# Three small edits around the second batch of a fused attention and gated-unit kernel: GpSimd makes the low part of Q, a product starts on three pairs of heads, a score buffer ends earlier

## The chip, the cores and the metric

One core of a Trainium2 chip. The time is device microseconds of one execution. The kernel before was run three times: 1341.32, 1342.89 and 1348.61 us, median 1342.89.

## The reference

Attention over 8 batches, 8 heads, 576 tokens, 64 features a head, in which only scores within `tau` of the row's maximum count; its output, 4608 tokens of 512 features, goes into a gated unit with 1536 inner features.

```
scores = q @ k.T / sqrt(64)
scores = where(scores >= max(scores) - tau, scores, -1e9)
x      = softmax(scores) @ v            # per batch and head, then heads side by side
gate   = sigmoid(x @ w_gate)
out    = (gate * (x @ w_val)) @ w_out
```

## The kernel before, in words

**Planner.** The kernel is a list of operations (`op`), each with an engine, an assumed cost, a key and the buffers it reads and writes. `Plan.run` (a list scheduler, executed while the program is built) lets every engine take the ready operation with the lowest key for which `room` finds free buffers; the instructions are then emitted in that order, so each engine's queue is fixed before the chip runs. `SLOTS` says how many buffers a tag has. An operation may also be tied `behind` another (it may be placed only once that one has been placed).

**Attention.** A visit is one pair of heads of one batch (8 batches of 4 pairs, 32 visits; counted from 0: pair 4 is the first pair of the second batch). A visit has nine score tiles: scores on PE (L653 or L661), maximum on DVE (L668), threshold on GpSimd or DVE (L677), exponential on ACT (L682), masking with the sum on DVE (L685), transposes on PE (L767) copied out of PSUM by ACT (L718), then the output product (L803). The first four pairs (`plain_scores`) use plain fp32. From pair 4 on (`split_scores`) K and Q are split in a rounded high part and the rest: ACT rounds K (L576) and scales and rounds Q (L578), GpSimd subtracts for K (L580), DVE for Q in one pass that scales and subtracts (L583). The parts are sent by SP into per-head tiles (`kd`, `qd`).

**Gated unit.** The output of a visit is split again (`split_x`, ACT L813 and GpSimd L815). When the four pairs of a batch are there, `in_units` computes 24 sums (12 blocks of gate and of value) of twelve matmuls each (four pairs of heads, three products each: L863), and `out_units` computes the second product (L906) with streamed weights (L841). A sum is issued in six chunks of two matmuls. Their keys start at 1e6, behind all attention. `FIRST_PAIRS` is the number of pairs that a chunk waits for at least: at 4 every chunk waits for all. The first three batches go through these two; the other five and a block of all leftover tokens are taken two at a time after attention (L1105, L1170), in a form with seven instead of eight products.

**Weights.** `convert` loads a piece of weights (SP, L473, L475), rebuilds its bits on GpSimd, ACT and DVE (L483, L487, L490, L496), and splits it (ACT L508, GpSimd L514). It shares the engines with attention until about 220 us.

**PSUM.** Eight banks: three double ones for scores (banks 0-1, 2-3, 4-5), two single ones (6, 7) for transposes, leftover keys, outputs and conversions. With the flag `active["moe"]` the third score buffer is given up and banks 4 and 5 become single banks; `started` sets it when the first product of the gated unit (key 1e6) is placed. While attention is active, the unit's sums may hold two single banks, attention two, conversions one.

Of the kernel before, what the change touches and what calls it, by code (L numbers as in the profile page):

```python
# [13 lines left out]
AF = mybir.ActivationFunctionType  # L14
ALU = mybir.AluOpType
# [5 lines left out]
def f32(ap):  # L21
    return ap.bitcast(F32)
# [21 lines left out]
class Plan:  # L44
# [51 lines left out]
        return o  # L96

    def room(self, o):
        need = {}
        for b in o.bufs + o.also:  # L100
            if b.tag in self.slots and not b.held:
                need.setdefault((b.tag, b.cls), set()).add(b)
        for (tag, cls), s in need.items():
            if len(s) + sum(len(x) for (t, c), x in need.items() if t == tag and c != cls) + self.held.get(
                tag, 0
            ) > self.slots[tag] - o.leave:
                return False
            cap = self.cap(tag, cls)
            if cap is not None and self.held.get((tag, cls), 0) + len(s) > cap:
                return False  # L110
            if tag in self.IN_TURN and any(b.turn != self.given.get(tag, 0) + 1 for b in s):
                return False
        if not self.settle([b for s in need.values() for b in s]):
            return False
        for s in need.values():
            for b in s:
                b.held = True
                self.given[b.tag] = b.turn
                self.held[b.tag] = self.held.get(b.tag, 0) + 1
                self.held[b.tag, b.cls] = self.held.get((b.tag, b.cls), 0) + 1  # L120
        return True

    def cap(self, tag, cls):
        return None

    def settle(self, bufs):

# [100 lines left out]
    "w": 9, "t2": 6,  # L228
}
LEAD = 8  # L230
CONV_IN, CONV_OUT = (24, 3), (56, 3)


# [48 lines left out]
def LATE(b, hp):  # L282
    return hp != 3

FIRST_PAIRS = 4
KD_COST = 1.2

TWOS = ((3, 4), (5, 6), (7, 8))
# [1 line left out]
SUMS_IN, SUMS_OUT, SUM_KEY = {1: (0,), 2: (1,)}, {0: (0,), 1: (1,)}, 300  # L290
# [8 lines left out]
def act(n):  # L299
    return 0.19 + 0.0008 * n  # L300
# [6 lines left out]
def pool(n):  # L307
    return 0.2 + 0.0022 * n


def mm(n):
    return 0.014 + 0.000418 * n
# [3 lines left out]
def kernel(  # L316
# [25 lines left out]
    nc = tc.nc  # L342
# [10 lines left out]
    SM = NJ * P  # L353
    SL = S - SM
    HALF = S // 2
    NF = DFF // P
    ND = DM // P
    NFG = NF // ND
# [24 lines left out]
    scale_t = cp.tile([P, 1], F32, tag="scale", name="scale_t")  # L383
# [16 lines left out]
    class Both(Plan):  # L400
# [23 lines left out]
                return more[0]  # L424
            return ps

        def started(self, o):
            if o.key == 1e6:
                active["moe"] = 1
            if o is last_att[0]:  # L430
                active["att"] = 0

# [2 lines left out]
    op, buf = plan.op, plan.buf  # L435
# [21 lines left out]
    def convert(i, f, key):  # L457
# [7 lines left out]
        raw = buf("w", [P, DM, 2], I32, f"wr{name}")  # L465
# [5 lines left out]
        def load():  # L471
# [4 lines left out]
                    out=raw.ap.rearrange("p f t -> p (f t)"), in_=w_out[f * P : (f + 1) * P, :]  # L476
                )

        op("SP", 1.6, key - 6, load, writes=[raw], leave=3)
        lo, hi = (lambda: raw.ap[:, :, 0]), (lambda: raw.ap[:, :, 1])  # L480

        bt = buf("b", [P, DM], F32, f"wb{name}", "conv")
# [1 line left out]
            out=at.ap.bitcast(F32), in0=hi().bitcast(F32), scalar1=zero_t[:, 0:1], scalar2=zero_t[:, 0:1],  # L484
# [44 lines left out]
    class Visit:  # L529
# [32 lines left out]
        def split_scores(self, key, n):  # L562
            b, hp = self.b, self.hp

            kn = buf("kn", [P, SK], F32, f"kn{n}")
            op("SP", 1.2, key - 6, lambda: nc.sync.dma_start(out=kn.ap, in_=k[b, hp]), writes=[kn])


            c0, c1 = self.c0, self.c1 + (2 * SL if self.with_left else 0)
            W, WM = c1 - c0, self.c1 - self.c0  # L570
            qn = buf("qn", [P, W], F32, f"qn{n}")
            op("SP", 1.2, key - 6, lambda: nc.sync.dma_start(out=qn.ap, in_=q[b, hp, :, c0:c1]), writes=[qn])


            k2 = self.k2 = buf("k2", [P, 2, SK + P], F32R, f"k2{n}")
            op("ACT", 0.73, key, lambda: nc.scalar.copy(k2.ap[:, 0, :SK], kn.ap), reads=[kn], writes=[(k2, 0)])  # L576
            q2 = self.q2 = buf("q2", [P, 2, W], F32R, f"q2{n}")
            op("ACT", act(W), key, lambda: nc.scalar.activation(q2.ap[:, 0], qn.ap, AF.Copy, scale=scale_t[:, 0:1]),  # L578
               reads=[qn], writes=[(q2, 0)])
            op("POOL", pool(SK), key, lambda: nc.gpsimd.tensor_tensor(  # L580
                out=k2.ap[:, 1, :SK], in0=kn.ap, in1=f32(k2.ap[:, 0, :SK]), op=ALU.subtract
            ), reads=[kn, (k2, 0)], writes=[(k2, 1)])
            op("DVE", 1.4 * W / 640, key, lambda: nc.vector.scalar_tensor_tensor(  # L583
                out=q2.ap[:, 1], in0=qn.ap, scalar=scale_t[:, 0:1], in1=f32(q2.ap[:, 0]), op0=ALU.mult, op1=ALU.subtract
            ), reads=[qn, (q2, 0)], writes=[(q2, 1)])
            self.WM = WM
            self.kd, self.qd = {}, {}
            for h in range(2):
                kd = self.kd[h] = buf("kd", [P, 2, SK], F32R, f"kd{n}_{h}")
                qd = self.qd[h] = buf("qd", [P, WM], F32R, f"qd{n}_{h}")  # L590
                own, other = slice(h * D, (h + 1) * D), slice((1 - h) * D, (2 - h) * D)
                for z, rows in enumerate((own, other)):
                    op("SP", 0.5, key + h, lambda qd=qd, rows=rows, own=own, z=z: nc.sync.dma_start(
                        out=f32(qd.ap[rows]), in_=f32(q2.ap[own, z, :WM])
                    ), reads=[(q2, z)], writes=[(qd, z)])
                for rows in (own, other):
                    op("SP", KD_COST, key + h, lambda kd=kd, rows=rows, own=own: nc.sync.dma_start(
                        out=f32(kd.ap[rows]), in_=f32(k2.ap[own, :, :SK])
                    ), reads=[k2], writes=[(kd, rows.start)])
# [228 lines left out]

    seq = [0]

    def moe_pe(cost, emit, reads, writes, also=()):
        seq[0] += 1
        return op("PE", cost, 1e6 + seq[0] - 1, emit, reads=reads, writes=writes, also=also)

    unit_ends = []

# [53 lines left out]

    def out_units(blk, g):

        two = blk in SUMS_OUT
        for es in ((0, 2), (1, 3)) if two else ((0,), (1,), (2,), (3,)):
            accs = {e: buf("b", [P, SM], F32, f"o{blk}_{e}", "moe") for e in es}
            outs = {e: buf("t2", [P, SM], F32, f"ot{blk}_{e}") for e in es}
            for fg, e in itertools.product(range(NFG), es):
# [4 lines left out]
                for j in range(0, 12, 2):  # L902
                    def go(j=j, w=w, fg=fg, acc=acc):
                        wv = w.ap.rearrange("p (f z c) -> p f z c", f=ND, z=2)
                        for f, a, z in ms[j : j + 2]:
                            nc.tensor.matmul(  # L906
                                acc.ap, wv[:, f, a], g[fg * ND + f].ap[:, z],
                                start=(fg, f, a, z) == (0, 0, 0, 0),
                                stop=(fg, f, a, z) == (NFG - 1, ND - 1, 1, 0),
                            )  # L910

                    fs = sorted({fg * ND + f for f, _, _ in ms[j : j + 2]})
                    end = moe_pe(2 * mm(SM), go, [g[f] for f in fs] + [w], [acc], also=[o] if fg == NFG - 1 else [])
                unit_ends.append(end)
                if e in SUMS_OUT.get(blk, ()):
                    first = w
# [470 lines left out]
```

## Time and profile before

| | |
|---|---|
| median of three runs | 1342.89 us (1341.32 to 1348.61) |
| profiled execution: span, first to last instruction | 1340.2 us (its device time is not given) |
| PE busy | 1314.8 us, 98% |
| DVE busy | 944.4 us, 70% |
| ACT busy | 727.8 us, 54% |
| GpSimd (POOL) busy | 492.7 us, 37% |
| DMA | 318.72 MB, mean 238 GB/s |

How to read it: PE is TensorE, PEld its weight loads, SPq the issuing of transfers. A row of a timeline is start (us), duration (us), engine, line, operation, output <- inputs, shapes, count merged in the row, and in brackets how long the engine was idle before it and what ended that. A row of the stage view is the stretch, its length, then for each engine busy us and number of instructions, and at its end the granted clock of TensorE as a share, the DMA share and GB/s. Matmuls are pipelined, so that neighbouring rows of PE overlap by some tenths.

### The profile page before, as it was taken

How to read it: one execution, taken by the hardware profiler on the slowest of the kernel's cores; microseconds unless marked ns; L12 is line 12 of the kernel's file. 1: busy time of each engine (PE TensorE's matmuls, PEld its weight loads, DVE VectorE, ACT ScalarE, POOL GpSimd, SP SyncE). 2: the span in 40 equal slices, each digit the busy share in tenths (PEclk: the TensorE clock that was granted, in tenths of full speed). 3: DMA queues.
4: the chain of work that ended last, by engine and by line, in shares of the span. 5: the costliest groups of instructions: out<-in, count | busy, mean ns of one | idle time of the engine just before them, and what ended most of it. 6: DMA issues, size and time to landing. Idle time of an engine off the chain costs nothing.

```text
span 1340.2 us, 23378 instructions
## 1 busy us (share of the span) xinstructions
PE 1314.8 (98%) x8292; PEld 1077.3 (80%) x8292; DVE 944.4 (70%) x1868; ACT 727.8 (54%) x1339; POOL 492.7 (37%) x474
## 2 busy tenths in 40 slices
PE   8889999999999999999999999999999999999998
PEld 5558887888888888888888888888888888888887
DVE  7888888777787776776777763556955569554594
ACT  8887777667767766666666652223522235322242
POOL 3576867724455363456464441110001010001100
PEclk9999999999999999999999999999999999999999
DMA  8889998999798888998988957656686566756563
GB/s 298 240 260 311 321 259 263 269 260 288 198 254 259 239 241 244 260 293 230 264 246 259 236 190 267 221 191 207 211 286 196 189 204 206 247 178 204 190 217 117
DMA packets 148115, 318.72 MB, mean 238 GB/s; under 512 B 28192, under 2 KB 56096, under 8 KB 148000
## 3 DMA queue, kind: packets, MB, share of 16 engines
q1 hardware_dynamic: 147856, 317.24, 78.3%
q8 instruction: 66, 1.08, 0.3%
q14 instruction: 49, 0.40, 0.1%
q10 hardware_dynamic: 144, 0.00, 0.0%
HBM read 211.16 MB, written 54.64 MB: 198 GB/s over the span
## 4 chain that ended last, share of the span: by engine, by line
PE 91%; DMA 4%; ACT 2%; POOL 1%; DVE 1%; issue 1%; SPq 0%; DVEq 0%; POOLq 0%; ACTq 0%
PE m L863 13%; PE qb L1105 11%; PE av L803 11%; PE s L661 8%; PE tp L767 8%; PE qc L1105 7%; PE qa L1105 7%; PE o L906 7%; PE rb L1170 5%; PE rc L1170 4%; PE ra L1170 4%; PE s_l L661 1%; PE tp_l L767 1%; PE s L653 1%; PE lk L780 1%
## 5 line engine op out<-in xcount | busy, mean ns | idle before, releaser
L668 DVE TENSOR_REDUCE st<-s 128x1 f32<-128x576 f32 x256 | 192.4, 753 | 83.2 <-PE s L661 76.0
L685 DVE SCALAR_TENSOR_TENSOR p<-s,st,p 128x576 f32<-128x576 f32 x256 | 206.5, 813 | 44.7 <-ACT p L682 39.4
L682 ACT ACTIVATE p<-s,st 128x576 f32<-128x576 f32 x256 | 191.1, 751 | 35.1 <-DVE st L668 34.4
L718 ACT COPY pt<-tp 128x512 f32<-128x512 f32 x256 | 149.4, 588 | 83.1 <-PE tp L767 79.1
L1018 POOL TENSOR_TENSOR gA<-gA 128x512 f32<-128x512 f32 x18 | 24.1, 1341 | 409.5 <-DVE gA L1084 409.5
L661 PE MATMUL s<-kd,qd 128*128 128x288 f32 x896 | 163.2, 306 | 2.6 <-DVE p_l L685 1.9
L863 PE MATMUL m<-x,wi 128*128 128x512 f32 x576 | 164.9, 405 | 0.0
L767 PE MATMUL tp<-ident,p 128*128 128x128 f32 x1024 | 155.4, 276 | 8.2 <-ACT pt L718 4.1
L767 PEld LDWEIGHTS tp<-ident,p 128*128 128x128 f32 x1024 | 119.8, 140 | 40.4 <-ACT pt L718 5.6
L661 PEld LDWEIGHTS s<-kd,qd 128*128 128x128 f32 x896 | 134.5, 189 | 13.4 <-DVE p_l L685 2.6
L803 PE MATMUL av<-pt,vs 128*64 128x256 f32 x1024 | 124.6, 385 | 0.8 <-ACT pt L718 0.8
L906 PE MATMUL o<-g,wo 128*128 128x512 f32 x432 | 120.4, 404 | 0.0
L1105 PE MATMUL qa<-xs_p,wa 128*128 128x512 f32 x432 | 109.4, 389 | 0.0
L1042 DVE TENSOR_TENSOR qu<-qb,qp 128x512 f32<-128x512 f32 x72 | 49.8, 692 | 82.5 <-PE qb L1105 71.2
L863 PEld LDWEIGHTS m<-x,wi 128*128 128x128 f32 x576 | 98.0, 189 | 12.0
L803 PEld LDWEIGHTS av<-pt,vs 128*64 128x64 f32 x1024 | 67.9, 136 | 48.5 <-issue 9.5
L1105 PEld LDWEIGHTS qa<-xs_p,wa 128*128 128x128 f32 x432 | 81.1, 188 | 16.8
L906 PEld LDWEIGHTS o<-g,wo 128*128 128x128 f32 x432 | 74.7, 189 | 10.0
L863 PE MATMUL m<-x,ws 128*128 128x512 f32 x288 | 78.5, 404 | 1.5 <-ACT pt L718 1.5
L887 POOL TENSOR_TENSOR g<-th,g 128x512 fp32r<-128x512 f32 x36 | 46.7, 1296 | 58.0 <-ACT g L885 57.8
L756 POOL TENSOR_SCALAR p<-p,zero_t,sm 128x576 f32<-128x576 f32 x64 | 56.5, 892 | 31.1 <-DVE sm L754 19.3
L1010 ACT CAST gs_p<-gA 128x512 fp32r<-128x512 f32 x54 | 32.8, 620 | 61.4 <-DVE gA L1084 23.0
(145 smaller groups left out, 2542.1 us busy)
## 6 DMA issues: line engine op xcount, KB each, us to landing
kd<-k SPq DMA_DIRECT2D x112, 320.0 KB
wi<-wid SPq DMA_DIRECT2D x48, 512.0 KB
wo<-wod SPq DMA_DIRECT2D x36, 512.0 KB
wa<-wid SPq DMA_DIRECT2D x36, 512.0 KB
ws<-sid SPq DMA_DIRECT2D x36, 512.0 KB
wt<-sid SPq DMA_DIRECT2D x36, 512.0 KB
wo_p<-sod SPq DMA_DIRECT2D x36, 512.0 KB
qd<-q SPq DMA_DIRECT2D x112, 128.0 KB
```

Of the source, the lines that this page charges most:

```text
L661: nc.tensor.matmul(s.ap[:, c, :HALF], st(), mv(slice(kc + c * HALF, kc + (c + 1) * HALF)), start=m == 0, stop=m == len(steps) - 1,)
L668: op("DVE", 0.76, key, lambda: nc.vector.tensor_reduce(out=st.ap[:, 0:1], in_=sv(), axis=AX.XY, op=ALU.max, negate=True), reads=[s], write ...
L682: op("ACT", 0.74, key, lambda: nc.scalar.activation(p(), sv(), AF.Exp, bias=st.ap[:, 0:1], scale=1.0), reads=[s, (st, 0)], writes=[(g.p, i)])
L685: op("DVE", 0.9, key, lambda: nc.vector.scalar_tensor_tensor(out=p(), in0=sv(), scalar=st.ap[:, 1:2], in1=p(), op0=ALU.is_ge, op1=ALU.mult ...
L718: return op("ACT", act(n), key, lambda: nc.scalar.copy(dst(), src.ap), reads=[src], writes=[part])
L756: op("POOL", 0.9, key, lambda i=i: nc.gpsimd.tensor_scalar(out=p.ap[:, i * S : (i + 1) * S], in0=p.ap[:, i * S : (i + 1) * S], scalar1=zer ...
L767: nc.tensor.matmul(tp.ap[:, c, :], self.p.ap[:, o + c * P : o + (c + 1) * P], ident, is_transpose=True, start=c == 0, stop=c == NJ - 1, sk ...
L803: nc.tensor.matmul(av.ap[h * D : (h + 1) * D, a:z], vis.vs.ap[:, j, h], m(h), start=i == 0, stop=i == len(ms) - 1, skip_group_check=True,)
L863: nc.tensor.matmul(m.ap, wv[:, a, c * P : (c + 1) * P], xs[c].ap[:, z, c0:c1], start=e == 0, stop=e == 11,)
L906: nc.tensor.matmul(acc.ap, wv[:, f, a], g[fg * ND + f].ap[:, z], start=(fg, f, a, z) == (0, 0, 0, 0), stop=(fg, f, a, z) == (NFG - 1, ND - ...
L1105: nc.tensor.matmul(acc.ap, wv[:, y, (2 * h + c) * P : (2 * h + c + 1) * P], xt[prod][c].get()[:, z], start=e == 0 and prod in FIRST, stop= ...
L1170: nc.tensor.matmul(acc.ap, w.ap[:, e, c, y], gt[prod][2 * g + c].get()[:, z], start=m == 0 and g == 0 and prod in FIRST, stop=m == 5 and g ...
```

## The change: what it does

- `Q_SPLIT = 8`: for pairs 4 to 7 ACT scales Q in place, a second ACT pass rounds it, and GpSimd subtracts. From pair 8 on all is as before.
- `FIRST_PAIRS = 3`: a chunk of a sum that needs only the first three pairs of heads no longer waits for the fourth. This holds in all blocks that go through `in_units`.
- `asked`: the flag that ends the third score buffer is set when the first product is looked at in `room`, whether or not it is placed then.
- The first chunk of `out_units` is placed only behind the last chunk of the block's `in_units`, and the first streamed weight load only behind the last load of gate and value weights.

```
     def room(self, o):
+        self.asked(o)
...
+Q_SPLIT = 8
...
-FIRST_PAIRS = 4
+FIRST_PAIRS = 3
...
-        def started(self, o):
+        def asked(self, o):
             if o.key == 1e6:
                 active["moe"] = 1
+
+        def started(self, o):
             if o is last_att[0]:
                 active["att"] = 0
...
-        op("SP", 1.6, key - 6, load, writes=[raw], leave=3)
+        loaded = op("SP", 1.6, key - 6, load, writes=[raw], leave=3)
+        if (f, i) == (NF - 1, 1):
+            last_load[0] = loaded
...
-            op("ACT", act(W), key, lambda: nc.scalar.activation(q2.ap[:, 0], qn.ap, AF.Copy, scale=scale_t[:, 0:1]),
-               reads=[qn], writes=[(q2, 0)])
+            by_pool = 4 * b + hp < Q_SPLIT
+            if by_pool:
+                op("ACT", act(W), key, lambda: nc.scalar.activation(qn.ap, qn.ap, AF.Copy, scale=scale_t[:, 0:1]),
+                   writes=[qn])
+                op("ACT", act(W), key, lambda: nc.scalar.copy(q2.ap[:, 0], qn.ap), reads=[qn], writes=[(q2, 0)])
+            else:
+                op("ACT", act(W), key, lambda: nc.scalar.activation(q2.ap[:, 0], qn.ap, AF.Copy, scale=scale_t[:, 0:1]),
+                   reads=[qn], writes=[(q2, 0)])
...
+            if by_pool:
+                op("POOL", pool(W), key, lambda: nc.gpsimd.tensor_tensor(
+                    out=q2.ap[:, 1], in0=qn.ap, in1=f32(q2.ap[:, 0]), op=ALU.subtract
+                ), reads=[qn, (q2, 0)], writes=[(q2, 1)])
+            else:
+                op("DVE", 1.4 * W / 640, key, lambda: nc.vector.scalar_tensor_tensor(
...
-        two = blk in SUMS_OUT
+        two, last = blk in SUMS_OUT, unit_ends[-1]
...
-                    end = moe_pe(2 * mm(SM), go, [g[f] for f in fs] + [w], [acc], also=[o] if fg == NFG - 1 else [])
+                    end = moe_pe(2 * mm(SM), go, [g[f] for f in fs] + [w], [acc], also=[o] if fg == NFG - 1 else [],
+                                 behind=last)
+                    last = None
```

## Rows read from the trace of the kernel before

**Rows 1.** Busy time of each engine by stage (columns above), whole core.
```profile
20.00:78.50 58.50, 51.89 (x440) 32.11 (x440) 51.93 (x108) 49.66 (x96) 35.38 (x53) 1.00 0.78 240
78.50:98.13 19.63, 14.92 (x128) 10.95 (x129) 17.50 (x36) 17.19 (x34) 15.89 (x17) 1.00 0.85 267
98.13:219.60 121.47, 118.76 (x829) 97.49 (x829) 103.58 (x209) 91.50 (x175) 81.83 (x74) 1.00 0.96 291
219.60:797.00 577.40, 574.82 (x4378) 481.23 (x4379) 425.69 (x988) 386.78 (x723) 298.04 (x273) 1.00 0.89 250
...
820.00:1340.20 520.20, 516.19 (x2278) 427.23 (x2276) 329.91 (x494) 163.68 (x281) 53.46 (x40) 1.00 0.63 207
```

**Rows 2.** Timeline of PE, 70 to 100 us.
```profile
79.12 1.06 PE L767 MATMUL tp<-ident,p 128*128 128x128 f32 x8 [1.07 <-ACT pt L718]
...
81.01 0.78 PE L661 MATMUL s<-kd,qd 128*128 128x288 f32 x4 [0.26 <-DMA xp<-xf]
...
86.63 0.63 PE L767 MATMUL tp<-ident,p 128*128 128x128 f32 x4 [0.77 <-ACT pt L718]
...
87.72 0.80 PE L661 MATMUL s<-kd,qd 128*128 128x288 f32 x4 [0.35 <-DVE p L685]
88.45 1.95 PE L803 MATMUL av<-pt,vs 128*64 128x256 f32 x16
...
98.13 2.11 PE L863 MATMUL m<-x,ws 128*128 128x512 f32 x8 [0.68 <-ACT pt L718]
```

**Rows 3.** Timeline of POOL, 55 to 125 us: low parts of x.
```profile
78.57 1.27 POOL L815 TENSOR_TENSOR x<-xf,x 128x512 fp32r<-128x512 f32 x1
...
92.62 1.28 POOL L815 TENSOR_TENSOR x<-xf,x 128x512 fp32r<-128x512 f32 x1 [1.53 <-ACT x L813]
```

**Rows 4.** Chain that ended last: start, us, what; 0 to 300 us.
```profile
157.41 3.64 PE m L863 x16
```

**Rows 5.** Timeline of DVE, 55 to 125 us.
```profile
86.85 0.81 DVE L685 SCALAR_TENSOR_TENSOR p<-s,st,p 128x576 f32<-128x576 f32 x1
```

**Rows 6.** Groups of instructions, 78.5 to 98.13 us: busy, mean ns, idle before.
```profile
L661 PE MATMUL s<-kd,qd 128*128 128x288 f32 x24 | 4.7, 318 | 0.6 <-DVE p L685 0.4 <-DMA xp<-xf 0.3
```

**Rows 7.** Timelines of DVE, 20 to 226 us: the low part of Q.
```profile
29.36 0.96 DVE L583 SCALAR_TENSOR_TENSOR q<-qn,scale_t,q 128x640 fp32r<-128x640 f32 x1
...
84.14 1.46 DVE L583 SCALAR_TENSOR_TENSOR q<-qn,scale_t,q 128x640 fp32r<-128x640 f32 x1
...
120.91 1.38 DVE L583 SCALAR_TENSOR_TENSOR q<-qn,scale_t,q 128x640 fp32r<-128x640 f32 x1
...
158.01 1.93 DVE L583 SCALAR_TENSOR_TENSOR q<-qn,scale_t,q 128x640 fp32r<-128x640 f32 x1
...
212.30 5.18 DVE L583 SCALAR_TENSOR_TENSOR q<-qn,scale_t,q 128x640 fp32r<-128x640 f32 x1
```

**Rows 8.** Timelines of ACT and POOL, 55 to 125 us: pair 5.
```profile
82.28 0.82 ACT L578 ACTIVATE q<-qn,scale_t 128x640 fp32r<-128x640 f32 x1
...
87.48 1.56 POOL L580 TENSOR_TENSOR k<-kn,k 128x640 fp32r<-128x640 f32 x1
```

**Rows 9.** Timelines of POOL and PE, 190 to 226 us.
```profile
211.95 0.83 POOL L483 TENSOR_SCALAR wa<-wr,zero_t 128x512 f32<-128x512 f32 x1
...
215.49 1.31 POOL L957 TENSOR_TENSOR s_o<-wo 128x512 f32<-128x512 f32 x1
...
219.60 0.80 PE L661 MATMUL s<-kd,qd 128*128 128x288 f32 x4 [1.91 <-DVE p_l L685]
```

**Rows 10.** Timeline of PE, 222 to 235 us.
```profile
231.48 0.62 PE L863 MATMUL m<-x,ws 128*128 128x512 f32 x2
...
233.01 1.98 PE L906 MATMUL o<-g,wo 128*128 128x512 f32 x8
```

**Rows 11.** Timeline of SP's issues, 200 to 260 us.
```profile
201.59 0.65 SPq L473 DMA_DIRECT2D wr<-in_moe_w_val_dram  x1
202.33 1.47 SPq L841 DMA_DIRECT2D wo<-wod  x1
```

More of the change, by code (lines that the diff above doesn't have):

```diff
@@ L124, in cap @@
         return None
+    def asked(self, o):
+        pass
     def settle(self, bufs):
@@ L425, in bank_pool, with asked @@
             return ps
-        def started(self, o):
+        def asked(self, o):
             if o.key == 1e6:
                 active["moe"] = 1
+        def started(self, o):
             if o is last_att[0]:
@@ L582, in split_scores @@
             ), reads=[kn, (k2, 0)], writes=[(k2, 1)])
-            op("DVE", 1.4 * W / 640, key, lambda: nc.vector.scalar_tensor_tensor(
-                out=q2.ap[:, 1], in0=qn.ap, scalar=scale_t[:, 0:1], in1=f32(q2.ap[:, 0]), op0=ALU.mult, op1=ALU.subtract
-            ), reads=[qn, (q2, 0)], writes=[(q2, 1)])
+            if by_pool:
[4 more added lines that the diff above has]
+                op("DVE", 1.4 * W / 640, key, lambda: nc.vector.scalar_tensor_tensor(
+                    out=q2.ap[:, 1], in0=qn.ap, scalar=scale_t[:, 0:1], in1=f32(q2.ap[:, 0]), op0=ALU.mult, op1=ALU.subtract
+                ), reads=[qn, (q2, 0)], writes=[(q2, 1)])
             self.WM = WM
@@ L829, with moe_pe @@
     seq = [0]
-    def moe_pe(cost, emit, reads, writes, also=()):
+    def moe_pe(cost, emit, reads, writes, also=(), behind=None):
         seq[0] += 1
-        return op("PE", cost, 1e6 + seq[0] - 1, emit, reads=reads, writes=writes, also=also)
+        return op("PE", cost, 1e6 + seq[0] - 1, emit, reads=reads, writes=writes, also=also, behind=behind)
     unit_ends = []
```

## The prediction

> **What bounds the kernel now.** First view: busy time of each engine by stage. From 98.13 us to 219.6 PE is busy 118.76 of 121.47 us, from 219.6 to 797 it is busy 574.82 of 577.40, and in the two-block tail 516.19 of 520.20; no other engine comes near that there (DVE 103.58 of 121.47, then 425.69 of 577.40) [rows 1]. So after 98 us TensorE is the bound, with 2.71 + 2.58 + 4.01 us of idle time in it. Only before 98 us is it not: 6.61 us idle between 20 and 78.5, and 4.71 us between 78.5 and 98.13 (19.63 less 14.92), where DVE is busy 17.50 and ACT 17.19 of 19.63 [rows 1]. The granted clock is 1.00, its 2.4 GHz level, in all these stages, so I put nothing on it.
>
> Second view: PE in order of time around that place. It waits again and again for an ACT copy that empties a transpose bank (1.07 and 0.77 us among others), once for DVE's last read of a score buffer (0.35), until the first product of the gated unit starts at 98.13, itself after a wait of 0.68 for such a bank [rows 2]. From there on there is always another product to run. The time of the kernel is therefore PE's work, plus its idle time; a change that takes no PE work away can only fill idle time. The ceiling of everything before 219.6 us outside the start is 6.61 + 4.71 + 2.71 = 14.0 us, one per cent.
>
> **The change part by part.**
>
> *Nine products on three pairs.* A product chunk is two matmuls, so a chunk that ends at the ninth product is still held by the fourth pair: what is set free in each sum are the chunks 0, 2, 4 and 6, eight matmuls of twelve. The low part of x of the third pair of batch 0 ends at 78.57 + 1.27 = 79.84, that of the fourth at 92.62 + 1.28 = 93.90 [rows 3]. So the unit can start some 14 us before the fourth pair is there, instead of 4.2 us behind it. While attention is active the unit may hold two banks, so two sums can run ahead: 16 matmuls. A matmul of 512 columns goes at 3.64 / 16 = 0.2275 us [rows 4], which gives 16 x 0.2275 = 3.64 us of PE work that moves from the full stage into the one with gaps. The gaps that it can use are those after 79.84: 4.71 less the 1.07 of the wait that ends at 79.12 [rows 1, 2], 3.64 us by coincidence. Not every chunk (0.46 us) fits a gap exactly, but what it displaces is attention work that is done later without loss; the part of the gaps after 93.90 is filled by ordinary chunks, as both sums can go on. Ends: 0 (no gap is hit) and -3.64; I take -3.0.
>
> *Early end of the third score buffer.* The flag falls now when the planner first looks at the first product, not when it places it. Banks 4 and 5 become single banks some 18 us sooner, and the scores have two buffers instead of three in that time. For PE this goes both ways. The waits for ACT's copies (0.77, 0.68) come from two single banks shared by transposes, leftover keys, outputs and weight conversions [rows 2], and with four they should mostly go: that is inside the 3.64 already. Against it, a score buffer is held long here: the score that starts at 81.01 is last read by the DVE pass that starts at 86.85 and takes 0.81, so 6.65 us [rows 2, 5]. Six score tiles start in the stage (24 matmuls of four a tile) [rows 6], one in 3.27 us; two buffers of 6.65 us give one in 3.33. I put the loss at 0 for that reason and price the other end as a rival.
>
> *Low part of Q of pairs 4 to 7 by GpSimd.* Four DVE passes go: 0.96, 1.46, 1.38 and 1.93 us, 5.73 us together [rows 7]. Four GpSimd subtractions come; the nearest row is the same operation on K with the same 128x640, 1.56 us, so 6.2 us. Four ACT passes come: now one scales Q (0.82 us), then there is a scaling in place and a copy, so one more of about 0.82 each, 3.3 us [rows 8]. After 98 us all three engines have slack against PE, which hides the sums: up to 219.6 ACT is idle for 121.47 - 91.50 = 30 us, GpSimd for 40, DVE for 18 [rows 1]. Of the four, two lie before 98 us (29.36 and 84.14). The first falls where PE idles 6.61 in 58.5 us and where thresholds of early tiles sit in GpSimd's queue; ends +1.56 (a threshold waits out the whole subtraction and PE with it) and -0.96 (DVE's pass was on the path). I take 0. The second is in the stage with the gaps: DVE's queue behind it held two conversions and then the very pass that PE's score at 87.72 waited for, 0.35 us [rows 2, 5, 7]. That gain is inside the 3.64 us too. The in-place scaling makes GpSimd's subtraction wait for two ACT passes instead of one; behind it on GpSimd stand low parts of weights, behind those SP's stores of them. Q is prepared eight tiles ahead of its use, so nobody on PE is near.
>
> What the row shows of the pass itself: alone it takes 0.96 us, and at 212.30 it took 5.18 while GpSimd worked without a gap from 211.95 to 216.80 (four instructions, the first and the last shown); PE's hole of 1.91 us before 219.60 stands behind it [rows 7 to 9]. That one is of a later pair and stays on DVE. The Trainium skill, "SBUF — State Buffer", section "SBUF: two separate sides", says that a DVE instruction with two SBUF inputs and a GpSimd instruction that reads SBUF exclude each other for whole instructions. The 5.18 us agree with it. It speaks against this part as much as for it: four passes lose their stalls, and those of later pairs meet 6.2 us more GpSimd work. Were the hole doubled by it, the sum would be -3.0 + 1.9 = -1.1 us, 1341.8, still inside the forecast's own range.
>
> For the hole, ends are -1.91 (GpSimd's run no longer meets the pass) and +1.91 (a second one). The order of all engines is written anew, so I take half a chance of its going: -0.6 with the 0.80 us or so of the rest of that stage.
>
> *Out behind in, and the loads behind the last weight.* The last product of the unit's first half ends before 232.2, the first of the second starts at 233.01 [rows 10]: already in that order. The wait now written down releases nothing later than it is; behind it on PE only work with a higher key stands. The streamed loads are now kept behind the last raw load of the gate and value weights on SP; that load is issued at 201.59 and the first streamed one at 202.33 [rows 11], so this order too is there already, and the note matters only if the new plan would have turned it round. Both 0, with ends of +-0.5 (about the 0.46 us of a chunk).
>
> *Everything after.* 2.58 us of idle time between 219.6 and 797 [rows 1] fall as the new order happens to fall: ends -2.6 and +2.6, taken as 0. The tail of 820 to 1340.2 is PE's and does not change.
>
> **Sum.** -3.0 - 0.6 = -3.6 us. Against the profiled span of 1340.2 that is 1336.6. Only the span of that execution is given, not its device time; the three runs took 1341.32, 1342.89 and 1348.61, so 1.1 us or more lie around the span, 2.7 by the median. I forecast 1342.89 - 3.6 = 1339.3 us, 0.27% less. A measurement of this kernel tells about 0.5% (6.7 us) from no change, so I call this the same.
>
> **Rivals.**
>
> *A. All the holes close.* The stage before 98 gives 3.64, that to 219.6 its 2.71, the middle 1 of its 2.58: -7.4 us, 1335.5; with something of the 6.61 before 78.5 too, 1333. For it: nearly all waits there are for banks or for a stalled DVE, and both are eased. Against: each part would have to come out at its end. Chance 0.21.
>
> *B. The third score buffer was worth more than the products.* Place: 79.84 to 98.13. If two buffers hold back attention, its PE work slips behind 98. A tile is 0.80 of scores, 0.66 of transposes and a quarter of 1.95 of output, 1.95 us [rows 2]. From 3.64 / 1.95 = 1.9 tiles on, the loss eats all of the moved products; with three of the six tiles slipped it is 5.85 - 3.64 = +2.2 us, 1345.1. For it: PE waited for exactly such a release at 87.72. Against: the computed pace, 3.33 against 3.27 us a tile, and PE has products to run once the fourth pair is in. Chance 0.13.
>
> *C. The change does not do what it says on the chip.* The planner's clock is its own costs; if there the fourth pair lands before PE has a free moment, or a bank is not free, the products stay where they are, and the flag's fall only swaps one wait for another: 1342.9, within 2 us. For it: priority to attention, whose keys are all lower. Against: PE idles in this stage in every few microseconds. Chance 0.20.
>
> *Forecast:* chance 0.46, own range 1336.5 to 1342.
>
> **How the numbers follow.** The range takes the forecast, C, most of A down to 1334 and B up to 1345; outside remains about a fifth of A, a third of B and the scatter of runs. Faster by over 0.5% means below 1336.2: most of A (0.17) and the edge of the forecast (0.04), 0.21. Slower by over 0.5% means above 1349.6: B with nearly all six tiles slipped (5.85 more), or several new holes like that of 219.60: 0.08. The rest, 0.71, is the same.
>
> **What would show it.** First product on PE near 80 to 83 us instead of 98.13, in two groups of eight, and a gap in the products until the fourth pair's x. PE idle between 78.5 and 98 near 1.5 instead of 4.71. No DVE pass on Q before 180 us, four more ACT passes and four more GpSimd subtractions of 128x640. Attention's end near 794 instead of 797. Wrong would be the forecast if PE's idle time outside 79 to 220 moved by more than 3 us, if the first product came no earlier, or if scores waited for DVE's last read more than 2 us in all in that stage.

## The result, and the profile after

The changed kernel takes 1350.29 us (median of 13 runs, 1346.15 to 1355.85) against 1342.74 (13 runs) for the kernel before: ratio 1.005, 95% interval 1.0033 to 1.0068. It is slower by about the 0.5% that I had set as the bound, and outside the range of 1334 to 1345. The profiled executions last 1348.5 us after and 1340.2 before.

First view: busy time by stage after the change, same columns and edges as [rows 1].

```profile
20.00:78.50 58.50, 53.26 (x448) 32.90 (x448) 51.23 (x108) 50.46 (x97) 36.80 (x56) 1.00 0.76 240
78.50:98.13 19.63, 17.94 (x145) 14.18 (x145) 16.37 (x35) 17.39 (x34) 16.96 (x17) 1.00 0.73 212
98.13:219.60 121.47, 116.36 (x798) 95.70 (x798) 100.88 (x213) 95.00 (x179) 85.66 (x77) 1.00 0.99 306
219.60:797.00 577.40, 567.53 (x4356) 474.65 (x4353) 417.80 (x970) 380.55 (x712) 293.50 (x268) 0.99 0.87 247
```

TensorE idles 5.24 us for 6.61 in the first of these stretches, 1.69 for 4.71 in the second: the change did there what it was to do. It then idles 5.11 for 2.71 and 9.87 for 2.58. The first two give 4.4 us, the last two take 9.7. The granted clock of the last one is 0.99, where it was 1.00.

The early part in order of time, TensorE and then GpSimd (start, duration, engine, line, operation, and the idle time before it):

```profile
87.63 0.71 PE L884 MATMUL m<-x,ws 128*128 128x512 f32 x2
...
91.68 2.57 PE L884 MATMUL m<-x,ws 128*128 128x512 f32 x10
...
94.62 0.63 PE L884 MATMUL m<-x,ws 128*128 128x512 f32 x2
```

```profile
89.55 1.57 POOL L600 TENSOR_TENSOR q<-qn,q 128x640 fp32r<-128x640 f32 x1
...
93.10 1.32 POOL L836 TENSOR_TENSOR x<-xf,x 128x512 fp32r<-128x512 f32 x1
```

Twelve products run from 87.63 us on, before the low part of the fourth pair's x (93.10, against 92.62 in [rows 3]); before, the first ran at 98.13 [rows 2]. Q's low part is on GpSimd, at 1.57 us. Of DVE's passes up to 220 us, two are left of which the first starts at 181.8 (tile view: count, then shortest, median and longest in ns):

```profile
L604 DVE SCALAR_TENSOR_TENSOR q<-qn,scale_t,q x2: 1551/1756/1961, 181.8 to 214.8; 128x640 fp32r<-128x640 f32 x2
```

To see where time is won and lost I added up TensorE's matmuls in order, each kind at its usual pace, and compared when the two executions had done the same sum. By this estimate after is 5.4 us ahead where the kernel before is at 159 us, 2.8 at 225, 0.2 at 351 and 477; then it is 4.6 behind at 540 and 9.9 behind at 603, 8.4 at the end. The largest steps lie at four holes. TensorE's rows there (the hole, and what ended it, in the brackets):

```profile
208.44 1.06 PE L788 MATMUL tp<-ident,p 128*128 128x128 f32 x8 [1.82 <-ACT xf L739]
...
287.76 1.95 PE L824 MATMUL av<-pt,vs 128*64 128x256 f32 x16 [1.71 <-ACT pl L739]
...
510.45 1.17 PE L788 MATMUL tp<-ident,p 128*128 128x128 f32 x8 [3.52 <-ACT pt L739]
...
589.85 1.12 PE L788 MATMUL tp<-ident,p 128*128 128x128 f32 x4 [3.83 <-POOL p L777]
```

Each is released by a short copy or scaling. What made that late stands in the queue of ScalarE or GpSimd just in front of it. ScalarE:

```profile
207.41 0.62 ACT L518 CAST ws<-wa 128x512 fp32r<-128x512 f32 x1 [2.33 <-DMA wod<-ws]
207.93 0.37 ACT L739 COPY xf<-av 128x256 f32<-128x256 f32 x1
...
286.92 0.62 ACT L834 CAST x<-xa 128x512 fp32r<-128x512 f32 x1 [2.99 <-DMA xa<-xa]
287.45 0.26 ACT L739 COPY pl<-lk 128x128 f32<-128x128 f32 x1
...
509.30 0.62 ACT L834 CAST x<-xa 128x512 fp32r<-128x512 f32 x1 [3.31 <-DMA xa<-xa]
509.82 0.58 ACT L739 COPY pt<-tp 128x512 f32<-128x512 f32 x1
```

GpSimd, before 589.85:

```profile
581.40 1.28 POOL L980 TENSOR_TENSOR s_o<-wo 128x512 f32<-128x512 f32 x1 [12.77 <-DMA sod<-s_o]
...
586.10 1.39 POOL L734 TENSOR_TENSOR xf<-xf,rb 128x576 f32<-128x576 f32 x1
587.46 1.53 POOL L596 TENSOR_TENSOR k<-kn,k 128x640 fp32r<-128x640 f32 x1
588.98 1.62 POOL L777 TENSOR_SCALAR p<-p,zero_t,sm 128x576 f32<-128x576 f32 x2
```

The pattern is the same in all four: an instruction that nobody needs soon (a weight cast, a copy of x for the next block, a sum of output weights) is reached before its transfer has landed. ScalarE and GpSimd ran in the order of their queues, as these rows show, so the copy that TensorE needs waited with it. (Each reading of a hole is from one profiled execution. The hole near 588 comes back in e5, e9 and e13 below, which keep TensorE's order there.)

The holes cost more than their length. Windows of 4 us, same columns as [rows 1], first after the change, behind the two longest holes, then before, behind its hole of 1.91 us [rows 9]:

```profile
508.00:512.00 4.00, 1.55 (x10) 1.46 (x11) 0.67 (x1) 2.70 (x6) 1.34 (x2) 0.92 0.73 288
512.00:516.00 4.00, 4.00 (x22) 2.42 (x22) 1.78 (x5) 2.11 (x4) 1.36 (x1) 0.66 0.82 178
516.00:520.00 4.00, 4.00 (x53) 3.73 (x50) 1.70 (x3) 1.96 (x5) 0.00 (x0) 1.00 0.85 192
...
588.00:592.00 4.00, 2.15 (x8) 1.85 (x9) 0.82 (x2) 0.87 (x2) 4.00 (x5) 0.73 0.69 187
592.00:596.00 4.00, 4.00 (x22) 3.22 (x21) 1.41 (x4) 2.25 (x5) 3.43 (x4) 0.84 0.98 214
```

```profile
220.00:224.00 4.00, 4.00 (x18) 3.52 (x17) 2.39 (x5) 2.25 (x5) 3.47 (x4) 0.57 0.94 202
224.00:228.00 4.00, 4.00 (x24) 3.37 (x24) 3.22 (x7) 1.83 (x3) 2.77 (x4) 1.00 0.92 273
```

Behind each, TensorE ran for a while at its lower level, 1.2 GHz. From 508 to 516 us that took (1 - 0.92) x 4 + (1 - 0.66) x 4 = 1.68 us of work, from 588 to 596 1.72, before from 220 to 224 1.72. So the hole of 3.52 us cost 5.2, that of 3.83 cost 5.5. The price differs from hole to hole: behind one of 4.29 us in e5 (below) the lower level took 3.4 us, twice as much. The lower level is also why PE is busy 1317.7 us for the same matmuls, 2.9 more than before. (A third such stretch after the change, 1.68 us between 8 and 16 us, is not of its making: 8 of the 19 profiles of this study show one in the first 20 us, among them e6, e14 and e15, which are made from the kernel before.)

Every run lists its mean granted clock. Time lost to the lower level, estimated as (1 - clock) x span, is 6.75 us in the mean over the 13 runs after, and 2.89 over the 130 runs of the kernel before that stand beside the experiments. (The 13 runs of it beside the result list no clock; their mean is 1343.90.) So of 6.1 us between the two means (1350.57 and 1344.48) 3.9 are clock and 2.2 are waits not made good by the early gain. Where the clock fell in the runs that were not profiled is not known.

### The profile page after: what moved, and what is told of

Its sections match the earlier page's. It is cut to its first block, busy times and chain, and to the rows that moved or that the text cites. A ratio compares the mean times of both kernels' runs of the same rounds, so it can differ in the third digit from the quotient of the medians.

```text
span 1348.5 us, 23387 instructions
## 1 busy us (share of the span) xinstructions
PE 1317.7 (98%) x8292; PEld 1079.3 (80%) x8292; DVE 938.1 (70%) x1864; ACT 730.6 (54%) x1343; POOL 499.8 (37%) x478
## 4 chain that ended last, share of the span: by engine, by line
PE 86%; DMA 6%; ACT 2%; DVE 2%; POOL 2%; issue 2%; SPq 1%; POOLq 0%; ACTq 0%; DVEq 0%
PE m L884 11%; PE qb L1128 11%; PE av L824 10%; PE tp L788 8%; PE s L682 7%; PE qa L1128 7%; PE qc L1128 7%; PE o L927 7%; PE rb L1193 5%; PE rc L1193 4%; PE ra L1193 4%; DMA qn<-in_q_dram 2%; PE s_l L682 1%; PE s L674 1%; PE lk L801 1%
## 5 line engine op out<-in xcount | busy, mean ns | idle before, releaser
L1041 POOL TENSOR_TENSOR gA<-gA 128x512 f32<-128x512 f32 x18 | 24.1, 1342 | 407.4 <-DVE gA L1107 407.4
L1103 ACT ACTIVATE gA<-qa 128x512 f32<-128x512 f32 x18 | 10.8, 598 | 100.6 <-PE qa L1128 100.6
```

## Experiments

Three theories. **L**: any new order of the queues draws anew which late transfers they stand on, several us either way. **Q**: the added ScalarE and GpSimd work itself brings the later holes. **P**: running ahead of the transfers brings them; that was tested last. All ratios are to the kernel before on the same chip. Every run computes the same as the kernel before unless its expectation says otherwise.

**Parts of the change.** e1 leaves out the Q part (`Q_SPLIT = 0`), e2 is the kernel before with the Q part alone, e3 the kernel before with `FIRST_PAIRS = 3` alone, e4 the Q part with the two orderings alone (`FIRST_PAIRS = 4`, the flag as before).

> The change without the Q edit (pairs 4 to 7 keep their low part on DVE). Theory L (order by luck: each new order leaves the in-order queues of ACT and GpSimd standing on other transfers that land later than the planner assumed): the gain of 3 to 5 us before 112 us stays, PE's holes after 190 us lie at other places, and the total is anywhere from -5 to +8 us against before. Rival Q (the extra ACT and GpSimd work of the Q edit makes the later holes): no holes over 2 us after 190 us, total 4 to 5 us under before, 1338. Rival P (the products that run ahead make transfers bunch later): holes of 10 us in all after 190 us as in the change, 1349.

> Only the Q edit. Theory L: no early gain (first product near 98 us), total within 6 us of before either way, with holes at places of its own. Rival Q: holes of about 8 to 10 us in all after 190 us, 1350 to 1352 (as the early gain is missing). Rival P: no new holes, as before within 2 us.

> Only nine products on three pairs (the flag's earlier fall changes nothing in this order of work). Theory L: early gain of 2 to 4 us, total anywhere from -5 to +8 us against before. Rival Q: 4 us under before. Rival P: as the change, 1349 to 1351.

> The Q edit with the fourth edit (out behind in, streamed loads behind the last weight), all four pairs needed and the flag as before. The planner gives the very same order for the change without the nine products, and for the change without the flag's earlier fall, so this run stands for all three. Theory L: no early gain, holes of its own, -5 to +8 us against before. Rival Q: 1350 to 1352. Rival P: as before within 2 us.

| | median us | ratio, 95% | PE idle 20-98 / 98-190 / 190-800 us |
|---|---|---|---|
| e1 | 1350.09 | 1.0041, 1.0023 to 1.0059 | 9.69 / 0 / 9.85 |
| e2 | 1348.5 | 1.0024, 1.0003 to 1.0046 | 8.47 / 0.58 / 9.00 |
| e3 | 1353.81 | 1.007, 1.0047 to 1.0093 | 9.69 / 0 / 12.60 |
| e4 | 1346.9 | 1.0014, 0.9995 to 1.0033 | 8.25 / 0.78 / 8.28 |
| after | 1350.29 | 1.005, 1.0033 to 1.0068 | 6.93 / 0 / 14.98 |
| before | | 1 | 11.20 / 0.93 / 4.49 |

No single part that was run is to blame, and the parts don't add up: the products alone cost 0.7%, the Q part alone 0.24%, and all together 0.5%. Many of the largest holes lie in other places each time (212.4 us in e1, 303.9 in e2, 247.5 in e3), but not all: e1 (586.8) and e2 (584.5) have the hole near 588 too, and behind the same addition, which waits for the same store. GpSimd, of e1 and then e2:

```profile
578.35 1.27 POOL L980 TENSOR_TENSOR s_o<-wo 128x512 f32<-128x512 f32 x1 [13.13 <-DMA sod<-s_o]
```

```profile
577.18 1.28 POOL L976 TENSOR_TENSOR s_o<-wo 128x512 f32<-128x512 f32 x1 [13.71 <-DMA sod<-s_o]
```

So a new order does not draw everything anew. Q falls as the sole cause, since e1 and e3 have none of that work and lose as much. P is not out yet: its times fit e1, e3 and e4, but not e2, which has no early products and still idles 9.00 us after 190. The fourth edit alone was not run: the order of each engine that the planner writes with it is that of the kernel before, line for line. Beside other edits it does write another order: e1 is e3 with it (the flag changes nothing there). The flag alone, which also writes an order of its own, was not run.

**The copies of x moved back.** e5 is the changed kernel's order with the four ScalarE casts of x each eight ScalarE instructions later and their GpSimd subtractions behind them, nothing else:

```
+        for o in [o for o in order if o.back]:
+            at = order.index(o)
+            own = [i for i in range(at + 1, len(order)) if order[i].eng == o.eng]
+            to = own[o.back - 1]
...
+            order.insert(to, order.pop(at))
...
+        if key == 0.5:
+            hi.back, lo.back = 8, 1
```

> The change's own order of work, with eight instructions moved: in the third batch, the four ACT copies of x that is read back from memory stand eight instructions later in ACT's queue, their four GpSimd subtractions behind them; every other instruction of every engine stands where it did. Theory L: PE's holes at 288 (1.71), 292 (0.71) and 510 us (3.52) go, with the low clock behind the last, and nothing else changes: 7 to 8 us less than the change, 1342 to 1344. Rival Q and rival P (the later holes come from load that the edits add, whatever the order): the waits only move to the next instruction, under 2 us less, 1348 or more.

1346.27 us, ratio 1.0011 (0.9992 to 1.003): above the 1342 to 1344 that L gave, below the 1348 of the rivals. By the ratios (1.0011 against 1.005) it gains 0.4%, about 5 us. Both holes that stood behind a cast of x are gone or small (1.11 us at 292). ScalarE near 510, where it had stood 3.31 us:

```profile
505.46 0.73 ACT L598 CAST k<-kn 128x640 fp32r<-128x640 f32 x1 [0.25 <-PE s_l L694]
506.09 0.58 ACT L751 COPY pt<-tp 128x512 f32<-128x512 f32 x1
...
510.12 0.64 ACT L846 CAST x<-xa 128x512 fp32r<-128x512 f32 x1
```

The copy of pt runs at 506.09, and the cast, at 510.12, finds its data there. By equal work this run gains 1.3 us at 287 and 5.1 at 510 on the changed kernel: hole and clock together. What it still loses is the hole near 588, here 4.29 us at 585.57, with a longer stretch at the lower clock behind it, (0.45 + 0.41) x 4 = 3.4 us of work:

```profile
584.00:588.00 4.00, 2.43 (x10) 2.13 (x11) 0.82 (x2) 0.59 (x2) 4.00 (x5) 0.55 0.71 205
588.00:592.00 4.00, 4.00 (x18) 3.32 (x17) 1.04 (x4) 2.25 (x5) 3.25 (x4) 0.59 0.96 233
```

**Constants that change nothing but the order.** e6 to e8 are the kernel before, e10 to e12 the changed kernel, each with one of the planner's costs changed by 1 to 7%: `KD_COST = 1.25` for 1.2 (e6, e10), 0.015 for 0.014 us in a matmul's cost (e7, e11), 0.00081 for 0.0008 in ScalarE's (e8, e12).

> The kernel before with one constant of the planner changed, the assumed cost of a K transfer 1.25 instead of 1.2; no operation is added, removed or given to another engine. Theory L: another order, other holes after 190 us, 3 to 10 us slower than before, like the change. Rivals Q and P, which lay the loss on the edits: as before within 3 us.

> The kernel before with the assumed cost of a matmul raised by 1 ns, nothing else. Theory L: another order, 0 to 10 us slower than before. Rivals Q and P: as before within 3 us.

> The kernel before with the assumed cost of an ACT pass raised by 5 ns at 512 columns, nothing else. Theory L: another order, 0 to 10 us slower than before. Rivals Q and P: as before within 3 us.

> The changed kernel with the planner's KD_COST 1.25 for 1.2; it computes the same. Theory L (the time of an order is a draw): this and the two runs beside it lie on both sides of 1345 us, spread over 1338 to 1353 us, with 3 to 15 us of PE idle time between 190 and 800 us. Rival S (the edits cost in the attention stage whatever the order, since the early part runs ahead of the transfers or the extra ScalarE and GpSimd work is there in every order): all three lie at 1346 to 1353 us, each with 8 to 15 us of PE idle time between 190 and 800 us.

> The changed kernel with 0.015 for 0.014 us as the planner's fixed cost of a matmul; it computes the same. Theory L: one more draw between 1338 and 1353 us, on either side of 1345. Rival S: 1346 to 1353 us with 8 to 15 us of PE idle time between 190 and 800 us.

> The changed kernel with 0.00081 for 0.0008 us as the planner's cost of a ScalarE element; it computes the same. Theory L: one more draw between 1338 and 1353 us, on either side of 1345; on the kernel before the same constant cost 7 us, and by L that says nothing of what it costs here. Rival S: 1346 to 1353 us, and above the changed kernel, as it was above the kernel before.

| constant | on the kernel before | on the changed kernel |
|---|---|---|
| none | 1 | 1350.29, 1.005 (1.0033 to 1.0068) |
| KD_COST | 1338.91, 0.996 (0.9939 to 0.998) | 1353.01, 1.007 (1.0044 to 1.0097) |
| matmul | 1344.86, 1.0016 (0.9991 to 1.0041) | 1348.62, 1.0038 (1.002 to 1.0056) |
| ScalarE | 1352.14, 1.0053 (1.0033 to 1.0073) | 1339.39, 0.9973 (0.9956 to 0.9991) |

The two columns cover much the same stretch, 0.996 to 1.0053 and 0.9973 to 1.007. One constant, which touches no instruction, moves the time as far as the change did. Their means are 1.0007 and 1.0033; with a scatter of 0.004 within each, four draws a side can't tell this 0.0026 from nothing. So S (all three of e10 to e12 at 1346 us and above) is out by e12, and L holds in this: the time scatters with the order, whatever writes it. That the edits make a good order somewhat rarer stays open.

L was not right in everything. For e6 it gave 3 to 10 us slower, and e6 is 0.4% faster. The idle time of e10 between 190 and 800 us (18.78) and of e12 (2.27) lies outside its 3 to 15. And e8 does not lose where L puts the holes: it idles 5.87 us between 190 and 800 (4.49 before), but 15.65 between 20 and 98 (11.20 before), where its clock is 0.95:

```profile
20.00:98.00 78.00, 62.35 (x495) 39.84 (x496) 65.37 (x130) 59.83 (x114) 48.19 (x65) 0.95 0.72 230
```

The fastest of either column, windows of 190 to 800 us, e6 and then e12:

```profile
190.00:800.00 610.00, 607.79 (x4623) 506.84 (x4622) 450.35 (x1038) 409.96 (x767) 320.62 (x294) 1.00 0.89 253
```

```profile
190.00:800.00 610.00, 607.73 (x4640) 506.77 (x4640) 450.63 (x1037) 410.90 (x769) 322.74 (x294) 1.00 0.86 249
```

Both idle 2.2 us there, and both beat the two kernels of this comparison.

**The hole near 588.** e9 is e5 with the five GpSimd additions at 581.40 (and the rest of that group) put behind the xf, K and p that stood behind them, and the group's two ScalarE casts behind the tenth ScalarE instruction counted from the group's first, which in effect is one place back; e17 counts 22 there in place of 10 and so puts the casts back twelve more.

```
+        pool = [o for o in order[first:] if o.eng == "POOL" and o not in mine][:5]
+        acts = [o for o in order[first:] if o.eng == "ACT" and o not in mine][:10]
...
+        to = order.index(pool[-1])
+        order[to + 1 : to + 1] = adds
...
+        to = max(order.index(acts[-1]), order.index(adds[-1]))
...
+        order[to + 1 : to + 1] = moved
```

> The changed kernel with the four copies of x moved back as in the run before, and one more group moved: the five GpSimd additions of the second output group's weight sums (one of them waited 12.77 us for a transfer to free its buffer, at 581.40 us) go behind the normalizing of xf, the subtraction for K and the three scalings of p that stood behind them, and the two ScalarE casts of the same sums ten ScalarE instructions back. Theory L (a hole is a queue that stands on a late transfer, and goes where the standing instruction goes): the hole of 4 us near 586 to 590 us is gone, no new one over 2 us after it, some 3.5 to 4 us less than with the copies alone: 1341 to 1344 us, PE idle of 6 to 7 us between 190 and 800 us. Rival M (the transfer itself is late and something must wait for it): the wait comes back within 30 us at another instruction, and the time stays at 1345 to 1348 us.

> The kernel of e9 (the changed kernel, the copies of x and the second output group's additions moved back) with the two ScalarE casts of that group another 12 ScalarE instructions back: in e9 the additions stood behind xf, K and p as intended, but ScalarE had reached the casts at 577.80 us and stood 6.28 us for those additions, and TensorE 5.07 us for the copy of pt behind them. Theory L (a hole is a queue that stands on something late): the hole near 586 us goes with the 1.7 us at the lower clock that follow it, PE idle between 190 and 800 us falls from 12.1 to 6 to 8 us, the median from 1348.0 to 1341 to 1344 us. Rival M (something near 586 us must wait, whichever instruction it is): a hole of 3 us or more within 30 us of it again, 1346 to 1349 us.

e9: 1347.99 us, ratio 1.0027 (1.0015 to 1.004), a miss. The hole was still there, behind the half of the group that I had not moved far enough. ScalarE, then TensorE, of e9:

```profile
577.38 0.43 ACT L767 COPY xf<-av 128x320 f32<-128x320 f32 x1 [1.71 <-PE av L852]
584.08 1.14 ACT L1022 CAST s_o<-s_o 128x512 fp32r<-128x512 f32 x2 [6.28 <-POOL s_o L1010]
```

```profile
586.39 0.47 PE L829 MATMUL lk<-ident,p 128*128 128x128 f32 x1 [5.07 <-ACT pt L767]
```

e17: 1343.29 us, ratio 0.999 (0.9977 to 1.0002). TensorE and its window, of e17:

```profile
587.00 0.66 PE L816 MATMUL tp<-ident,p 128*128 128x128 f32 x4 [0.81 <-POOL p L805]
...
593.16 0.65 PE L816 MATMUL tp<-ident,p 128*128 128x128 f32 x4 [1.55 <-POOL p L805]
```

```profile
190.00:800.00 610.00, 601.57 (x4587) 501.63 (x4587) 447.85 (x1038) 407.79 (x763) 322.98 (x296) 1.00 0.89 253
```

```profile
219.60:797.00 577.40, 574.27 (x4408) 480.04 (x4404) 423.13 (x988) 385.92 (x722) 299.10 (x274) 1.00 0.88 250
```

No hole over 2.1 us is left in these stretches, their clock is 1.00, and the profiled span is 1339.2 against 1348.5. Between 219.60 and 797 TensorE idles 3.13 us (9.87 in the changed kernel, 2.58 before). Between 190 and 800 it idles 8.43, a little over the 6 to 8 that L gave. TensorE's and DVE's orders are those of the changed kernel, SP's too but for one issue; six instructions on ScalarE and eleven on GpSimd were put elsewhere. That is the whole loss against the kernel before, with the change left in; the gain that I had forecast it does not bring. M falls. What remains are the three holes at 202 to 216 us (1.04, 2.01, 1.63), the middle one behind the weight cast that waits for its store, as at 207.41 above; they were not moved.

**Is a lead worth its length?** The orders kept, TensorE's work shifted by 24 matmuls (5.46 us): e13 the changed kernel and e15 the kernel before with two sums computed twice, e14 the kernel before and e16 the version e12 with eight products of three sums left out. The first two lines below are of e13 and e15, the last two of e14 and e16.

```
+                        if again and j + step == 12:
+                            for e in range(12):
...
+                            if few and 2 <= e < 10:
+                                continue
```

> The changed kernel, every queue in its order, with one addition: TensorE computes the first two sums of the gated unit twice (24 matmuls of 0.2275 us, 5.46 us, near 96 and 104 us), which takes away the 5.4 us by which it ran ahead of the kernel before at 112 us. Theory P (work done ahead of the transfers that bound 100 to 220 us and load the attention stage is lost again later): the later waits shrink by what is added, PE idle between 190 and 800 us falls from 15 to about 10 us, and the time stays within 1.5 us of the changed kernel's 1350.3. Theory L (the holes belong to the order alone): they stay, 1355 to 1356 us. A share between tells how much of the lead was lost to P.

> The kernel before, every queue in its order, with 24 matmuls (products 3 to 10 of the first three sums of the gated unit) left out, so those sums are not the reference's: TensorE gets 5.46 us ahead near 98 to 110 us, as it did in the changed kernel, without any new order. Theory P: the lead is lost again, PE idle between 190 and 800 us rises from 4.5 to 8 to 10 us and the time is 1340 to 1343 us. Theory L: the order of before has few holes and keeps most of the lead, 1337 to 1338 us.

> The kernel before with the first two sums of the gated unit computed twice: 24 more matmuls, 5.46 us late near 104 to 112 us. Theory L: nothing absorbs it but part of the hole of 1.91 us at 219.60 and small waits after it: 1346.5 to 1348.5 us. Theory P: the transfers were the bound there before too, and the delay is taken up by the 6 us of waits after 98 us: 1343 to 1345 us.

> The version of the changed kernel with 0.00081 in the planner's ScalarE cost (1339.4 us; it is 2.4 us behind the kernel before at 159 us and has 2.3 us of PE idle time between 190 and 800 us), in its order, with the same 24 matmuls left out, so three sums are not the reference's: 5.46 us less work near 100 us. Theory L: it stays free of holes and gains 4 to 5.5 us, 1334 to 1335.5 us. Theory P: it gets ahead of the transfers like the changed kernel, idle time between 190 and 800 us rises to 5 to 8 us, and the time is 1337 to 1340 us.

| | median us | ratio, 95% | by L / by P |
|---|---|---|---|
| e13 | 1354.0 | 1.0078, 1.0054 to 1.0101 | 1355 to 1356 / 1348.8 to 1351.8 |
| e14 | 1342.68 | 1.0006, 0.9986 to 1.0025 | 1337 to 1338 / 1340 to 1343 |
| e15 | 1353.25 | 1.0064, 1.0041 to 1.0086 | 1346.5 to 1348.5 / 1343 to 1345 |
| e16 | 1342.32 | 0.9993, 0.9978 to 1.0007 | 1334 to 1335.5 / 1337 to 1340 |

Neither theory foretold the four. More work costs: e15 at least the length of what was added; for e13, against the changed kernel's 1.005, the intervals leave anything from nothing to somewhat more than that length. Less work gains nothing (e14 against the kernel before; e16 against e12's 0.9973). PE idle time between 190 and 800 us is 12.88, 3.78, 6.62 and 2.18 us in e13 to e16. P wanted 10 in e13 (L 15) and a rise to 8 to 10 in e14 and to 5 to 8 in e16: half right in e13, wrong in the two others, though the time of e14 lies in its range. In e13 the hole at 510 us is gone with the cast of x left where it stood. ScalarE comes to it some 5 us later (its cast of K just before starts at 510.65, in the changed kernel at 505.25) and finds the data landed:

```profile
511.29 0.62 ACT L834 CAST x<-xa 128x512 fp32r<-128x512 f32 x1
```

Other holes of e13 have grown (2.48 us at 292.98, 4.96 at 591.31). So the order alone does not fix the holes; when an engine comes to the standing instruction counts too.

Windows of 98 to 190 us, kernel before, then e14:

```profile
98.00:190.00 92.00, 91.07 (x633) 75.01 (x634) 77.19 (x161) 71.64 (x138) 61.98 (x54) 1.00 1.00 301
```

```profile
98.00:190.00 92.00, 86.77 (x607) 69.76 (x608) 78.70 (x160) 71.27 (x137) 61.02 (x55) 1.00 1.02 307
```

Without the 24 matmuls TensorE idles 5.23 us there for 0.93, at once and not later as P had it, waiting for copies of ScalarE and a read of DVE (1.8 and 1.4 us the largest sums). So in e14 something other than TensorE's work sets the time of that stretch, and the products only fill it. The DMA share is 1.0 there; whether the transfers or the attention chain set the pace was not separated.

## Why the prediction was wrong

- *What bounds the kernel.* "The time of the kernel is therefore PE's work, plus its idle time" is only bookkeeping: e14 takes 5.46 us of work out, more of the stretch becomes idle, and the time stays. So work moved into an early gap need not shorten the whole.
- *Nine products.* The stage did as forecast: idle 1.69 us between 78.5 and 98.13 (forecast near 1.5), no wait of a score for DVE's p in it. But the first products came at 87.63, not 80 to 83, and twelve of them before the fourth pair's x, not two groups of eight: the size came out, the way to it only in part. The early gain was 5.4 us by 159 us, more than the 3.0 + 0.6 taken. But that is a lead, not time saved.
- *Third score buffer* (rival B): B's place, 79.84 to 98.13, shows no loss, as said. What the flag does alone was not run.
- *Low part of Q.* Right that four DVE passes go and that the sums hide before 98 us: the Q part alone (e2) idles 8.47 us between 20 and 98, the kernel before 11.20. (The 0.96 us that I took for a pass alone was not quite alone: GpSimd's subtraction before it ended at 29.64. The shortest pass after the change takes 0.88.) The hole at 219.60 did go. In its place stand 1.04, 1.82 and 1.64 us at 202 to 216: +2.4 for that stage where I had -0.6.
- *Out behind in.* 0 alone, as said: it leaves every order as it was. Beside the other edits it is one more redraw (e1 against e3: 1.0041 and 1.007, 9.85 and 12.60 us of idle time after 190).
- **The step that failed** is *Everything after*: "2.58 us of idle time between 219.6 and 797 [rows 1] fall as the new order happens to fall: ends -2.6 and +2.6, taken as 0". It measured +7.3 us of idle time between 219.60 and 797, and two falls of the clock (3.4 us) where the kernel before had one (1.7). With the two standing groups moved (e17) that stretch idles 3.13 us and the loss is gone. Term by term, from the profiles: -3.0 us between 78.5 and 98.13 (forecast -3.0), -1.4 before that (0), +2.4 to 219.6 (-0.6), +7.3 to 797 (0), +2.9 of busy time at the lower clock (0), +8.2 of the 8.3 us between the spans. I had bounded a redraw by what the old order happened to hold, though an order with few holes has little idle time to lose and much to take on. A better bound (argued, not tested) was what one standing instruction can cost: in the trace of the kernel before, GpSimd waits 14.05 us for a load of wo until 527.73, and TensorE happens to be busy all the while. The chance of 0.08 for slower was too small by far: of the eleven orders other than the one before with no work moved by hand (after, e1 to e4, e6 to e8, e10 to e12), four are slower by 0.5% or more and none faster by as much.
- *The clock.* "The granted clock is 1.00, its 2.4 GHz level, in all these stages, so I put nothing on it": the mean of a stage of 577 us hid the 1.7 us behind the hole at 219.60, and so the price of any new hole.
- My own sign of being wrong came true: "if PE's idle time outside 79 to 220 moved by more than 3 us". It moved by 7.3 after 219.60.

## What to carry to other kernels

Where a planner writes the order of every queue, an edit of a few us is one draw among orders that scatter by more than the edit is worth, here 0.996 to 1.007: run it with two or three neutral changes of a cost on both sides before calling it good or bad. Then look in the profile for short instructions that TensorE needs, standing behind a cast or a sum that waits for a transfer; moving two such groups by up to 13 places gave back 0.6%. Price a hole with the slower clock behind it, and do not count filler moved into an early gap as time saved.

## What was not expected of the hardware

- A hole of 3.52 us cost 5.2: the granted clock went to 1.2 GHz behind it, and 1.7 us of work were lost. Behind one of 4.29 us in e5 it was 3.4 us. In the runs the lower clock makes up 3.9 of the 6.1 us between the kernels. Behind the holes of 1.64 to 1.82 us of the changed kernel it stayed at 1.00; behind the one of 1.91 in the kernel before it fell to 0.57 from 220 to 224 us.
- The same kernel's runs differ in part by this: over 130 runs of the kernel before, time rises 1.1 us for each us of (1 - clock) x span, with the clock from 0.992 to 1.0. The correlation is 0.67, so that just under half of the variance goes with the clock.
